# Reordering one iteration of a banded attention loop: P·V and x^T ahead of layer norm and weight conversion, a weight's halves behind the transposes' eviction, and 1e-9 added on ScalarE

## The chip, the cores and the metric

The kernel runs on one core of a Trainium2 chip. The metric is the device time of one execution in microseconds (us). The engines are TensorE (PE in the rows; PEld is its weight load), VectorE (DVE), ScalarE (ACT), GpSimd (POOL) and SyncE (SP), which issues nearly all DMAs. Each runs its own instructions strictly in the order in which the program lists them.

## The reference

Three steps follow one another, for 2 batches, 768 positions and a model width of 512:

```python
scores = scale * np.matmul(q, k.transpose(0, 1, 3, 2))        # 8 heads of 64
scores = np.where(is_sink | in_window, scores, -1e9)           # window 128, 4 sinks
scores = scores - np.max(scores, axis=-1, keepdims=True)
a = np.exp(scores)
a = a / (np.sum(a, axis=-1, keepdims=True) + 1e-09)
x = np.matmul(a, v)                                            # -> (2, 768, 512)

h = np.maximum(x @ w_in, 0.0)                                  # d_ff 1024
u, v = h[..., :512], h[..., 512:]
v_n = (v - mean(v)) / np.sqrt(var(v) + 1e-06)
gated = u * (einsum('ts,bsd->btd', w_spatial, v_n) + b_spatial)
x = gated @ w_out

h = np.maximum(x.transpose(0, 2, 1) @ w_tok1, 0.0) @ w_tok2
u = x + h.transpose(0, 2, 1)
out = u + np.maximum(u @ w_ch1, 0.0) @ w_ch2
```

## The kernel before

The matrix products behind attention run as three products each: every operand is kept as a high half (rounded by a ScalarE copy) and a low half (the difference, on GpSimd or VectorE), and `mm3` (line 55) multiplies high·high, high·low and low·high. The weights arrive in double precision; `pump` (466) turns a 128x512 piece into single precision with three VectorE instructions (lines 481, 485, 488), and `flush` (496) makes its halves, the high one on ScalarE (499), the low one on GpSimd (500). `pump` flushes the piece converted before it.

Attention is a software pipeline, `banded` (339). Block j is 128 query rows of one batch, and group g = 2j + ph is four of its eight heads. Iteration n runs from -3 to 25 and works on several groups at once. Group n+1 has its sums inverted (`sums`, 190) and its exponentials scaled (`norm`, 239: two heads on GpSimd, two on ScalarE). Group n is transposed on TensorE into one bank `tr` (`a_transpose`) and evicted by ScalarE (aT) and VectorE (aL) (`a_out`, 271). Group n+3 gets its scores (`qk`, `scores`), and group n+2 its exponentials (`expo`, 223). Group n-1 is multiplied with the values (`pv`, 288) into the one bank `pv`, which holds a whole block. In an even iteration block j-1 is finished by `sinks_mm`, and `x_out` (325) splits it: the high half xTH on ScalarE, the low half xTL on VectorE. Only then may `pv` start the next block in that bank. The sink columns take a path of their own (`v_step`, `sink_parts`, `sinks`, and `split_vs` for the sinks' values, in iterations 1 and 13).

Everything behind attention that can start early is woven in: `step` (426) moves layer norms one stage on, `pump` converts one piece of `w_in` in each of iterations -1 to 6 (`PUMPS`), and `fill` (433) puts up to about 1900 ns of later matmuls behind each iteration on TensorE, as soon as the x^T that they read is written and only in the iteration after that. The order of calls in the loop is the order on each engine:

```python
if n in (1, 13):
    self.split_vs(n // 12)
self.step()
if n in PUMPS:
    self.pump()
...
if 0 <= n - 1 < NG:
    self.pv(n - 1)
    if ph == 0:
        ...
        self.x_out(j - 1)
```

Attention ends near 143 us; `mlp` (663) follows with the leftover fills, the spatial product, and the token and channel MLPs.

Of the kernel before, what the change touches and what calls it, by code (L numbers as in the profile page):

```python
# [8 lines left out]
F32R = mybir.dt.float32r  # L9
I32 = mybir.dt.int32  # L10
U32 = mybir.dt.uint32
AF = mybir.ActivationFunctionType
ALU = mybir.AluOpType
PSUM = bass.MemoryType.PSUM

P = 128
B, H, S, D = 2, 8, 768, 64
NB = S // P
DM = H * D
# [5 lines left out]
SK = 8  # L25
SR = 3 * 4 * SK
# [3 lines left out]
NG = B * NB * 2  # L30
# [6 lines left out]
def f32(ap):  # L37
    return ap.bitcast(F32)


class Kernel:
# [106 lines left out]
            nc.sync.dma_start(out=raw[0:SR], in_=self.vs[b])  # L148
            self.vsraw = raw

    def split_vs(self, b):

        nc = self.nc
        raw = self.vsraw
        t = self.vsb[b] = self.ap.tile([P, DM], F32R, name="vs", tag="vs", bufs=1)
        nc.scalar.activation(out=t[0:SR], in_=raw[0:SR], func=AF.Copy)
        r = slice(4 * SK, 8 * SK)
        nc.vector.tensor_tensor(out=t[r], in0=raw[r], in1=f32(t[r]), op=ALU.subtract)

    def slots(self, j):  # L160

# [28 lines left out]
    def sums(self, g):  # L190

        V = self.nc.vector
        r = self.ap.tile([P, 4], F32, name="r", tag="r", bufs=3)
        self.rs[g] = r
        V.tensor_scalar(out=r, in0=self.sm[g], scalar1=1e-9, scalar2=None, op0=ALU.add)
        V.reciprocal(r, r)

    def scores(self, g):

# [23 lines left out]
    def expo(self, g):  # L223
        nc = self.nc
        j, ph = divmod(g, 2)
        i = j % NB
        u = KW if i else P
        s, nm = self.ss[g]
        if ph == 0:
            self.e[j] = self.ap.tile([P, H, KW], F32, name="e", tag="e", bufs=2)  # L230
        sm = self.ap.tile([P, 4], F32, name="sums", tag="sums", bufs=3)
        self.sm[g] = sm
        for c in range(4):
            nc.scalar.activation(  # L234
                out=self.e[j][:, 4 * ph + c, :u], in_=s[:, c, :u], func=AF.Exp, bias=nm[:, c : c + 1], scale=-1.0,
                accum_out=sm[:, c : c + 1],
            )

    def norm(self, g):

        nc = self.nc
        j, ph = divmod(g, 2)
        r = self.rs[g]
        w = KW if j % NB else P
        e = self.e[j][:, 4 * ph : 4 * ph + 4, 0:w]
        nc.gpsimd.tensor_tensor(
            out=e[:, 2:4], in0=e[:, 2:4], in1=r[:, 2:4].unsqueeze(2).to_broadcast([P, 2, w]), op=ALU.mult
        )
        for c in range(2):
            nc.scalar.activation(out=e[:, c], in_=e[:, c], func=AF.Copy, scale=r[:, c : c + 1])  # L250

    def sink_parts(self, j):

# [85 lines left out]
    def banded(self):  # L339
        self.q, self.vb, self.vsb, self.ps_s, self.ss, self.e, self.sm, self.rs = {}, {}, {}, {}, {}, {}, {}, {}  # L340
        self.aT, self.ps_x, self.aS, self.dv, self.eS = {}, {}, {}, {}, {}
        NJ = B * NB
        self.kr = self.ap.tile([P, NC4, RING, KW], F32, name="kr")
        self.vf = self.ap, "vf", 2
        self.scalar_loads(self.cp)
        self.load_qk(0, 2)
        self.warm(10)
        self.load_qk(1)
        self.prefetch()
        self.load_v(0)  # L350
        self.load_qk(2)
        self.masks(self.ap)
        for n in range(-LQ, NG + 2):
            j, ph = divmod(n, 2)
            self.xdone = self.xnext
            if ph and n >= -1:
                if (n + 7) // 2 < NJ:
                    self.load_qk((n + 7) // 2)
                if (n + 3) // 2 < NJ:
                    self.load_v((n + 3) // 2)  # L360
            if 0 <= n + LN < NG:
                self.sums(n + LN)
            if 0 <= n < NG:
                self.a_transpose(n)
                self.a_out(n)
            if 0 <= n + LN < NG:
                self.norm(n + LN)
            if n + LQ < NG:
                self.qk(n + LQ)
                if n < 0:  # L370
                    self.warm(3)
                self.scores(n + LQ)
            if 0 <= n + LE < NG:
                self.expo(n + LE)
            if 0 <= n < NG and ph == 0 and j % NB:
                self.v_step(j)
                self.sink_parts(j)
            if n in (1, 13):
                self.split_vs(n // 12)
            self.step()  # L380
            if n in PUMPS:
                self.pump()
            if n == max(PUMPS) + 1:
                self.flush()
            if 0 <= n - 1 < NG:
                self.pv(n - 1)
                if ph == 0:
                    if (j - 1) % NB:
                        self.sinks_mm(j - 1)

                    self.fill_until(j - 1)
                    self.x_out(j - 1)
            if 0 <= n < NG and ph == 1 and j % NB:
                self.sinks(j)
            if n == NG - 4:
                self.raws = [self.spatial_load(r) for r in range(2)]
            self.fill(BUDGET)
        self.xdone = self.xnext
        self.vf = self.sp, "tmp", 4
# [529 lines left out]
```

## Time and profile before

| | before |
|---|---|
| median of 3 runs | 494.08 us (492.68 to 495.11) |
| profiled execution, its own time | 494.1 us |
| its span, first to last instruction | 492.3 us |
| PE busy | 469.2 us (95%) |
| PEld busy | 392.3 us (80%) |
| DVE busy | 281.2 us (57%) |
| ACT busy | 178.8 us (36%) |
| POOL busy | 146.7 us (30%) |
| mean granted TensorE clock | 0.979 |

The profile lists the busy time of each engine by stretch, the chain of work that ended last (followed back from the end to what released each step), groups of instructions by line, and a timeline. A row of the timeline has start, duration, engine, line, operation, tiles written and read, and in brackets the idle time ahead of it with its releaser. A granted clock of 1.00 is 2.4 GHz, 0.50 is 1.2 GHz. 1.8 us of the profiled execution lie outside the span.

### The profile page before, as it was taken

To read this page: it belongs to the slowest core of one execution; us is meant where nothing else is said; L and a number is where in the kernel's file an instruction comes from. 1 tells how busy PE (TensorE), PEld (TensorE's weight loads), DVE (VectorE), ACT (ScalarE), POOL (GpSimd) and SP (SyncE) were. 2 spreads that over 40 slices of the span, in tenths; PEclk is the share of its full clock that TensorE was granted. 3 is DMA by queue.
4 is the path that set the end of the run, shared out by engine and by line. 5 is a ranking of instruction groups with operands and counts; after the bars stand their busy time and mean duration, and the time that the engine had idled before them with its cause. 6 is when DMAs were issued, how large, how long until landed. Compare 5 with 4: busy or idle time off the path is not lost.

```text
span 492.3 us, 6952 instructions
## 1 busy us (share of the span) xinstructions
PE 469.2 (95%) x2562; PEld 392.3 (80%) x2562; DVE 281.2 (57%) x633; ACT 178.8 (36%) x483; POOL 146.7 (30%) x164
## 2 busy tenths in 40 slices
PE   8678899999999999999999989999999999999994
PEld 7356588788898999998888768888888888888883
DVE  5899865775555399937878698666412211311112
ACT  4656777787754323225642122222101210010000
POOL 1355752354354556642543033222100000000000
PEclk9859899999999999999999999999999999999998
DMA  8744132202005023303534044222010000200002
GB/s 258 246 151 152 66 101 95 87 22 87 1 30 185 1 85 87 102 6 116 173 119 137 35 129 128 91 94 73 21 66 1 0 1 0 86 1 0 1 0 92
DMA packets 19722, 38.48 MB, mean 78 GB/s; under 512 B 1824, under 2 KB 8224, under 8 KB 19680
## 3 DMA queue, kind: packets, MB, share of 16 engines
q1 hardware_dynamic: 19248, 37.69, 23.5%
q8 instruction: 22, 0.36, 0.3%
q10 hardware_dynamic: 432, 0.26, 0.2%
q14 instruction: 20, 0.16, 0.1%
HBM read 34.80 MB, written 3.15 MB: 77 GB/s over the span
## 4 chain that ended last, share of the span: by engine, by line
PE 81%; DVE 11%; ACT 5%; issue 1%; POOL 1%; POOLq 0%; ACTq 0%
PE pso L60 7%; PE pso L58 7%; PE pso L59 7%; PE psc L58 6%; PE psc L60 6%; PE psc L59 6%; PE psg L60 3%; PE psg L59 3%; PE psg L58 3%; PE pv L301 3%; PE ps L60 2%; PE ps L58 2%; PE ps L59 2%; ACT e L234 2%; DVE wi L485 2%; PE psu L58 2%
## 5 line engine op out<-in xcount | busy, mean ns | idle before, releaser
L647 DVE SCALAR_TENSOR_TENSOR hh<-psc,hh 128x512 fp32r<-128x512 f32 x36 | 24.9, 691 | 124.6 <-ACT hh L646 124.6
L646 ACT ACTIVATE hh<-psc 128x512 fp32r<-128x512 f32 x36 | 21.5, 597 | 156.0 <-PE psc L60 156.0
L60 PE MATMUL pso<-c2H,hh 128*128 128x512 f32 x144 | 56.3, 391 | 1.9 <-DVE hh L647 1.9
L58 PE MATMUL pso<-c2H,hh 128*128 128x512 f32 x144 | 56.8, 394 | 0.0
L59 PE MATMUL pso<-c2L,hh 128*128 128x512 f32 x144 | 56.1, 390 | 0.0
L488 DVE SCALAR_TENSOR_TENSOR wi<-rawi,wi 128x512 int32<-128x512 int32 (+2 forms) x46 | 40.3, 876 | 1.6
L234 ACT ACTIVATE e<-s,nm 128x136 f32<-128x136 f32 (+1 forms) x96 | 37.6, 393 | 3.9 <-DVE nm L218 3.9
L485 DVE SCALAR_TENSOR_TENSOR wi<-rawi,wi 128x512 int32<-128x512 int32 (+2 forms) x46 | 36.4, 791 | 1.6
L481 DVE TENSOR_SCALAR wi<-rawi 128x512 int32<-128x512 int32 (+2 forms) x46 | 33.4, 726 | 0.7 <-DMA rawi<-in_moe_w_ch 0.5
L60 PEld LDWEIGHTS pso<-c2H,hh 128*128 128x128 f32 x144 | 27.0, 188 | 8.0 <-DVE hh L647 2.3
L58 PE MATMUL psg<-wsTH,vnH 128*128 128x384 f32 x96 | 32.1, 334 | 0.0
L59 PE MATMUL psg<-wsTL,vnH 128*128 128x384 f32 x96 | 32.1, 334 | 0.0
L60 PE MATMUL psg<-wsTH,vnL 128*128 128x384 f32 x96 | 32.1, 334 | 0.0
L500 POOL TENSOR_TENSOR c2L<-wi,c2H 128x512 fp32r<-128x512 f32 x12 | 16.1, 1339 | 52.4 <-ACT c2H L499 52.4
L59 PEld LDWEIGHTS pso<-c2L,hh 128*128 128x128 f32 x144 | 27.1, 188 | 5.4
L58 PEld LDWEIGHTS pso<-c2H,hh 128*128 128x128 f32 x144 | 27.0, 188 | 5.3
L188 PE MATMUL sc<-kr,q 64*128 64x264 f32 (+2 forms) x192 | 28.8, 419 | 0.4 <-DVE nm L218 0.2
L60 PE MATMUL psc<-u2H,c 128*128 128x512 f32 x72 | 28.0, 389 | 0.0
L58 PE MATMUL psc<-u2H,c1H 128*128 128x512 f32 x72 | 28.0, 389 | 0.0
L59 PE MATMUL psc<-u2L,c1H 128*128 128x512 f32 x72 | 28.0, 389 | 0.0
L60 PE MATMUL psc<-u2H,c1L 128*128 128x512 f32 x72 | 28.0, 389 | 0.0
L58 PE MATMUL psc<-u2H,c 128*128 128x512 f32 x72 | 28.0, 389 | 0.0
(143 smaller groups left out, 1120.1 us busy)
## 6 DMA issues: line engine op xcount, KB each, us to landing
rawi<-in_moe_w_ch SPq DMA_DIRECT2D x24, 512.0 KB, 3.4
rawi<-in_moe_w_in SPq DMA_DIRECT2D x8, 512.0 KB, 4.5
v<-in_v SPq DMA_DIRECT2D x12, 256.0 KB, 3.6
out_x<-o SPq DMA_DIRECT2D x12, 256.0 KB, 2.4
kr<-in_k SPq DMA_DIRECT2D x11, 272.0 KB, 4.1
q<-in_q SPq DMA_DIRECT2D x11, 256.0 KB, 4.2
raws<-in_w_spT SPq DMA_DIRECT2D x6, 384.0 KB, 4.5
rawi<-in_moe_w_out SPq DMA_DIRECT2D x4, 512.0 KB, 5.2
```

Of the source, the lines that this page charges most:

```text
L58: self.nc.tensor.matmul(ps, lh, rh, start=(first and i == 0), stop=False)
L59: self.nc.tensor.matmul(ps, lh, rl, start=False, stop=False)
L60: self.nc.tensor.matmul(ps, ll, rh, start=False, stop=(last and i == n - 1))
L188: nc.tensor.matmul(o, q[r, p, :], k, start=True, stop=True)
L234: nc.scalar.activation(out=self.e[j][:, 4 * ph + c, :u], in_=s[:, c, :u], func=AF.Exp, bias=nm[:, c : c + 1], scale=-1.0, accum_out=sm[:, ...
L301: nc.tensor.matmul(ps[h * D : (h + 1) * D, p, :], w[:, (2 * p + h) * D : (2 * p + h + 1) * D], self.aT[g][c][:, 2 * x + h, :], start=(p == ...
L481: V.tensor_scalar(out=wi, in0=hi, scalar1=3, scalar2=0x3FFFFFFF, op0=ALU.logical_shift_left, op1=ALU.bitwise_and,)
L485: V.scalar_tensor_tensor(out=wi, in0=hi, scalar=-0x40000000, in1=wi, op0=ALU.bitwise_and, op1=ALU.bitwise_or)
L488: V.scalar_tensor_tensor(out=wi, in0=lo, scalar=29, in1=wi, op0=ALU.logical_shift_right, op1=ALU.bitwise_or)
L500: self.nc.gpsimd.tensor_tensor(out=dl, in0=w, in1=f32(dh), op=ALU.subtract)
L646: nc.scalar.activation(out=h, in_=ps, func=AF.Relu)
L647: nc.vector.scalar_tensor_tensor(out=l, in0=ps, scalar=0.0, in1=f32(h), op0=ALU.max, op1=ALU.subtract)
```

## The change

Four things in one iteration, all in `banded` and its helpers:

- `pv(n-1)`, `sinks_mm` and `x_out` stand ahead of `v_step`, `sink_parts`, `split_vs`, `step` and `pump`, instead of behind them.
- The piece converted in iteration n-1 is flushed right behind `a_out` and the GpSimd part of `norm`, ahead of the ScalarE part of `norm`; `pump` then finds nothing to flush.
- `sums` is the reciprocal alone; the 1e-9 is added by a ScalarE copy with a bias at the end of `expo`.
- `split_vs` is in two parts: ScalarE's in iterations 2 and 14, VectorE's in 3 and 15.

```diff
-    def split_vs(self, b):
+    def split_vs(self, b, part):
...
-        t = self.vsb[b] = self.ap.tile([P, DM], F32R, name="vs", tag="vs", bufs=1)
-        nc.scalar.activation(out=t[0:SR], in_=raw[0:SR], func=AF.Copy)
-        r = slice(4 * SK, 8 * SK)
-        nc.vector.tensor_tensor(out=t[r], in0=raw[r], in1=f32(t[r]), op=ALU.subtract)
+        if part == 0:
+            t = self.vsb[b] = self.ap.tile([P, DM], F32R, name="vs", tag="vs", bufs=1)
+            nc.scalar.activation(out=t[0:SR], in_=raw[0:SR], func=AF.Copy)
+        else:
+            t = self.vsb[b]
+            r = slice(4 * SK, 8 * SK)
+            nc.vector.tensor_tensor(out=t[r], in0=raw[r], in1=f32(t[r]), op=ALU.subtract)
...
-        V.tensor_scalar(out=r, in0=self.sm[g], scalar1=1e-9, scalar2=None, op0=ALU.add)
-        V.reciprocal(r, r)
+        V.reciprocal(r, self.sm[g])
...
+        nc.scalar.activation(out=sm, in_=sm, func=AF.Copy, bias=1e-9)
...
             if 0 <= n + LN < NG:
-                self.norm(n + LN)
+                self.norm(n + LN, "P")
+            if n - 1 in PUMPS:
+                self.flush()
+            if 0 <= n + LN < NG:
+                self.norm(n + LN, "A")
             if n + LQ < NG:
...
                 self.expo(n + LE)
-            if 0 <= n < NG and ph == 0 and j % NB:
-                self.v_step(j)
-                self.sink_parts(j)
-            if n in (1, 13):
-                self.split_vs(n // 12)
-            self.step()
-            if n in PUMPS:
-                self.pump()
-            if n == max(PUMPS) + 1:
-                self.flush()
             if 0 <= n - 1 < NG:
                 self.pv(n - 1)
...
                     self.x_out(j - 1)
+            if 0 <= n < NG and ph == 0 and j % NB:
+                self.v_step(j)
+                self.sink_parts(j)
+            if n in (2, 3, 14, 15):
+                self.split_vs(n // 12, n % 2)
+            self.step()
+            if n in PUMPS:
+                self.pump()
```

The order on TensorE and on the DMA queues does not change. Three places where it does, as the built programs list it.

VectorE, from the last scores of iteration 2 to the first transposes' low copy of iteration 3, before:

```order
L218 ISA s,nm<-sc,m_141 128x136
L218 ISA nm 128x1
L481 TENSOR_SCALAR wi<-rawi 128x512
L485 SCALAR_TENSOR_TENSOR wi<-rawi,wi 128x512
L488 SCALAR_TENSOR_TENSOR wi<-rawi,wi 128x512
L330 TENSOR_TENSOR xTL<-pv,xTH 128x4x128
L195 TENSOR_SCALAR r<-sums 128x4
L196 RECIPROCAL r<-r 128x4
L278 TENSOR_TENSOR aL<-tr,lowT 128x512
```

and now:

```order
L220 ISA s,nm<-sc,m_141 128x136
L220 ISA nm 128x1
L335 TENSOR_TENSOR xTL<-pv,xTH 128x4x128
L488 TENSOR_SCALAR wi<-rawi 128x512
L492 SCALAR_TENSOR_TENSOR wi<-rawi,wi 128x512
L495 SCALAR_TENSOR_TENSOR wi<-rawi,wi 128x512
L198 RECIPROCAL r<-sums 128x4
L283 TENSOR_TENSOR aL<-tr,lowT 128x512
```

The low half of x^T (xTL) has moved ahead of the three conversions, and the addition ahead of the reciprocal is gone.

ScalarE in iteration 4 (aT is the transposes' eviction, wuH a weight's high half, e<-e,r the scaling, sums the exponentials' sums), before:

```order
L275 ACTIVATE aT<-tr 128x512
L250 ACTIVATE e<-e,r 128x136 x2
L234 ACTIVATE e,sums<-s,nm 128x136 x4
L257 ACTIVATE eS<-e 128x2x32
L499 ACTIVATE wuH<-wi 128x512
L329 ACTIVATE xTH<-pv 128x4x128
L532 ACTIVATE vf<-psv 128x512
```

and now:

```order
L280 ACTIVATE aT<-tr 128x512
L506 ACTIVATE wuH<-wi 128x512
L255 ACTIVATE e<-e,r 128x136 x2
L236 ACTIVATE e,sums<-s,nm 128x136 x4
L240 ACTIVATE sums<-sums 128x4
L334 ACTIVATE xTH<-pv 128x4x128
L262 ACTIVATE eS<-e 128x2x32
L539 ACTIVATE vf<-psv 128x512
```

The weight's high half has moved from behind the exponentials to ahead of the scaling, the addition of 1e-9 is new, and xTH stands ahead of the sinks' copy eS.

GpSimd in iteration 2 (e<-e,r is its part of the scaling, dv the difference of two value blocks, wvL a weight's low half), before:

```order
L246 TENSOR_TENSOR e<-e,r 128x272
L285 TENSOR_TENSOR dv<-v 128x512
L258 CAST eS<-eS 128x2x32
L259 TENSOR_TENSOR eS<-e,eS 128x2x32
L500 TENSOR_TENSOR wvL<-wi,wvH 128x512
```

and now:

```order
L250 TENSOR_TENSOR e<-e,r 128x272
L507 TENSOR_TENSOR wvL<-wi,wvH 128x512
L290 TENSOR_TENSOR dv<-v 128x512
L263 CAST eS<-eS 128x2x32
L264 TENSOR_TENSOR eS<-e,eS 128x2x32
```

The weight's low half is now second in the iteration instead of last; in odd iterations GpSimd's order stays as it was.

## Rows read from the trace of the kernel before

**Rows 1.** Busy time by stretch: us, each engine's busy us (instructions), granted clock, DMA share, GB/s.

```profile
10.00:60.00 50.00, 37.93 (x253) 26.48 (x252) 46.62 (x148) 32.90 (x119) 26.04 (x30) 0.83 0.51 168
20.00:35.00 15.00, 10.73 (x54) 7.12 (x55) 13.42 (x45) 10.32 (x38) 6.92 (x9) 0.54 0.47 157
60.00:150.00 90.00, 89.16 (x696) 73.75 (x695) 53.39 (x206) 64.07 (x214) 40.68 (x60) 1.00 0.20 66
```

**Rows 2.** Pieces of the chain that ended last: start, us, what.

```profile
31.10 1.98 PE pv L301 x16
...
54.53 0.61 DVE xTL L330
55.18 1.85 PE pv L301 x16
...
60.27 0.44 PE tr L267 x4
```

**Rows 3.** TensorE's longest wait between 9 and 60 us: us, times, longest.

```profile
PE pv L301 <- DVE xTL L330: 4.2, 3, 1.6
```

**Rows 4.** Line 195 alone, by stretch: us, VectorE's busy us (instructions), granted clock, DMA.

```profile
14.00:54.50 40.50, 2.65 (x7) 0.83 0.52 171
```

**Rows 5.** Groups by line on VectorE, 9 to 60 us: count, busy us, mean ns, idle.

```profile
L488 DVE SCALAR_TENSOR_TENSOR wi<-rawi,wi 128x512 int32<-128x512 int32 x8 | 7.5, 935 | 0.3
L485 DVE SCALAR_TENSOR_TENSOR wi<-rawi,wi 128x512 int32<-128x512 int32 x8 | 6.5, 815 | 0.3
...
L481 DVE TENSOR_SCALAR wi<-rawi 128x512 int32<-128x512 int32 x8 | 4.5, 559 | 0.0
```

**Rows 6.** The same eight conversions by tile: duration ns min/median/max.

```profile
L481 DVE TENSOR_SCALAR wi<-rawi x8: 421/426/1427, 12.3 to 52.6; 128x512 int32<-128x512 int32 x8
L485 DVE SCALAR_TENSOR_TENSOR wi<-rawi,wi x8: 691/692/1658, 12.8 to 53.1; 128x512 int32<-128x512 int32 x8
L488 DVE SCALAR_TENSOR_TENSOR wi<-rawi,wi x8: 691/693/1676, 13.5 to 53.8; 128x512 int32<-128x512 int32 x8
```

**Rows 7.** Timeline, 17 to 28 us: GpSimd beside VectorE.

```profile
17.48 1.75 POOL L500 TENSOR_TENSOR wvL<-wi,wvH 128x512 fp32r<-128x512 f32 x1 [2.19 <-ACT wvH L499]
...
18.02 1.23 DVE L195 TENSOR_SCALAR r<-sums 128x4 f32<-128x4 f32 x1
...
22.39 0.68 DVE L158 TENSOR_TENSOR vs<-vsraw,vs 32x512 fp32r<-32x512 f32 x1 [1.13 <-ACT vs L156]
...
26.95 1.27 POOL L285 TENSOR_TENSOR dv<-v 128x512 f32<-128x512 f32 x1
...
27.22 0.30 DVE L218 CUSTOM_DVE_ANT_0 s<-sc,m 128x136 f32<-128x136 f32 x1
```

**Rows 8.** Timeline of iteration 4 on ScalarE and VectorE.

```profile
37.09 0.18 DVE L196 RECIPROCAL r<-r 128x4 f32<-128x4 f32 x1
37.36 0.71 ACT L250 ACTIVATE e<-e,r 128x136 f32<-128x136 f32 x2
37.98 0.39 ACT L234 ACTIVATE e<-s,nm 128x136 f32<-128x136 f32 x1
...
39.54 0.24 ACT L257 ACTIVATE eS<-e 128x64 fp32r<-128x64 f32 x1
39.69 0.62 ACT L499 ACTIVATE wuH<-wi 128x512 fp32r<-128x512 f32 x1
39.87 0.49 DVE L481 TENSOR_SCALAR wi<-rawi 128x512 int32<-128x512 int32 x1
40.21 0.57 ACT L329 ACTIVATE xTH<-pv 128x512 fp32r<-128x512 f32 x1
```

**Rows 9.** Timeline: TensorE's longest idle time between 60 and 150 us.

```profile
69.29 0.44 PE L58 MATMUL psu<-xTH,wuH 128*128 128x384 f32 x1 [0.57 <-ACT aS L313]
```

**Rows 10.** Timeline of TensorE, 26 to 31 us: transposes and scores of iteration 3.

```profile
26.99 1.09 PE L267 MATMUL tr<-ident,e 128*128 128x128 f32 x4 [3.29 <-DVE aL L278]
28.01 2.13 PE L188 MATMUL sc<-kr,q 64*128 64x264 f32 x8
```

More of the change, by code (lines that the diff above doesn't have):

```diff
@@ L237, in expo, with norm @@
             )
-    def norm(self, g):
+        nc.scalar.activation(out=sm, in_=sm, func=AF.Copy, bias=1e-9)
+    def norm(self, g, on):
         nc = self.nc
@@ L245, in norm @@
         e = self.e[j][:, 4 * ph : 4 * ph + 4, 0:w]
[L246 to L250, printed above, removed]
+        if on == "P":
+            nc.gpsimd.tensor_tensor(
+                out=e[:, 2:4], in0=e[:, 2:4], in1=r[:, 2:4].unsqueeze(2).to_broadcast([P, 2, w]), op=ALU.mult
+            )
+        else:
+            for c in range(2):
+                nc.scalar.activation(out=e[:, c], in_=e[:, c], func=AF.Copy, scale=r[:, c : c + 1])
     def sink_parts(self, j):
```

## The prediction, made before the changed kernel ran

> **What bounds the kernel now.** I read busy time by stretch first, then the chain of waits, then the timeline where the chain changes engine. By stretch [rows 1], TensorE works 89.2 of the 90 us from 60 to 150, so there it is the bound and nothing that other engines save can show. From 10 to 60 us it works 37.9 of 50, while VectorE works 46.6 of 50: the early attention iterations are VectorE's, and TensorE has no other work yet, since the products behind attention need x^T. The clock says the same: between 20 and 35 us the granted clock is 0.54, mostly the lower of the two levels, 1.2 GHz. The chain of waits [rows 2] runs mostly over VectorE up to 54.53 us, where VectorE writes the third low half of x^T (xTL); that releases the bank `pv`, and TensorE takes over at 55.18 with the next block's products with the values. From its transposes at 60.27 TensorE has work without end. TensorE's longest wait before that is of this kind: `pv` for xTL, three times, 4.2 us [rows 3].
>
> So the question is by how much the third xTL, the one of iteration 6, comes earlier. From there TensorE needs 60.27 - 54.53 = 5.7 us to the point where it is saturated, and the rest of its work follows unchanged, because its order is unchanged.
>
> **The change part by part**, on VectorE's path up to that xTL (iterations 0 to 6).
>
> *1e-9.* Line 195 goes. Seven of its instructions lie on the path and take 2.65 us [rows 4]. They are 128x4 elements; one took 1.23 us, from 18.02 to 19.25, while GpSimd's low half of a weight ran from 17.48 to 19.23 [rows 7]. VectorE stood still until GpSimd was done. The reciprocal now comes first in the iteration and could stand still in its place; then little more than the 7 x 0.16 = 1.1 us of unhindered ones would be saved (0.16 is an estimate from the reciprocal's 0.18 [rows 8], with the same shape). But GpSimd's work moves too (next part), so I take **-2.65**, bounds -1.1 and -2.65.
>
> *A weight's halves behind the eviction.* The eight conversions take 7.5 + 6.5 + 4.5 = 18.5 us [rows 5]; unhindered, by their medians, 8 x (0.693 + 0.692 + 0.426) = 14.5 [rows 6]. So 4.0 us are standing still, in single instructions of 1.4 to 1.7 us, and the cause is the one above: GpSimd subtracts the last weight while VectorE converts the next. In the changed order GpSimd subtracts right after its part of the scaling, while VectorE evicts transposes and masks scores. There the two do not hinder each other: dv on GpSimd took 1.27 and the masking beside it 0.30 [rows 7], the time of dv elsewhere. Behind the weight's low half GpSimd has dv (1.27) and the sinks, and later a layer norm's low half, and these reach into the conversions of iterations 2, 4 and 6; I give back 0.5. **-3.5**, bounds 0 (it stays, beside another instruction) and -4.0.
>
> *Sinks' values in two parts.* VectorE waited 1.13 us for ScalarE [rows 7]; with an iteration between the parts the wait goes, the 0.68 of work stays: **-1.1**.
>
> *x^T ahead of the conversion.* The conversion of iteration 6 (0.426 + 0.692 + 0.693 [rows 6]) now lies behind the third xTL: **-1.8** for TensorE. But VectorE works in order, so xTL in front of the conversion waits for xTH, where before the conversion filled that time. In iteration 4 [rows 8] scaling began 0.27 after the reciprocal, took 0.62, the exponentials 1.56. Now the weight's high half (39.69 to 40.21: 0.52) stands ahead of the scaling, and it cannot start before the last conversion, which ends about where the reciprocal starts. So xTH starts 0.1 + 0.52 + 0.62 + 1.56 + the addition after the reciprocal, and ends 0.57 later. The addition on ScalarE is new: the nearest row is the sinks' copy, 0.24 long with the next instruction 0.15 behind it; an exponential (1.56 / 4 = 0.39) bounds it above, 0.1 below; I take 0.2, near the small copy. xTH ends 3.6 after the reciprocal, while VectorE is free after 39.87 - 37.09 = 2.8, less 0.2 if nothing keeps its eviction waiting: a wait of 0.8 to 1.0. Three times: **+3.0**, bounds 2.1 and 4.0.
>
> The Trainium skill speaks against putting the addition there: ScalarE: Activation LUTs, "Rules for kernel authors", sends adds to VectorE and budgets about 0.3 us for an ACTIVATE, with a pointer as bias (the bias here is a constant). By that figure the three additions on the path would cost 0.3 us more in all, an estimate from that page; the trace shows no ACTIVATE of this shape.
>
> Sum to the third xTL: -2.65 - 3.5 - 1.1 - 1.8 + 3.0 = -6.05.
>
> *What is late next.* TensorE comes 6 us earlier, VectorE less: the conversion and layer norm of iteration 6 still stand ahead of its next reciprocal. In iteration 9 TensorE waited 0.57 us for the sinks' eviction aS, which ScalarE does behind the exponentials [rows 9]; it now finds aS behind the addition as well, and behind a scaling that is released later relative to it. I put **+0.6** there, bounds 0 and 1.5. Later additions lie on ScalarE, which works 64 of 90 us from 60 to 150 [rows 1], and cost nothing while TensorE is the bound there. dv behind a weight costs nothing: it is read an iteration later. The DMA queues keep their order.
>
> Net -5.45: the profiled execution took 494.1 us, as the median of the runs (494.08), so **488.6 us**.
>
> **The rivals.**
>
> *VectorE keeps the pace (490.5).* If not the 5.7 us of TensorE's work but VectorE's next reciprocal and ScalarE's scaling set the time of the saturation, the 1.8 us of the conversion behind xTL are no gain: 494.1 - 4.25 + 0.6 = 490.5. For it: TensorE ran part of these 5.7 us at the lower clock, as `pv` with 1.85 beside 1.98 shows [rows 2], and could be faster, hence waiting again. Against it: 5.7 us hold the 0.6 of xTL, 1.8 of conversion and 0.9 to the end of the scaling with room to spare. Chance 0.17.
>
> *The standing still stays (493.7).* If GpSimd holds VectorE up wherever its work is put, or the reciprocal inherits it, only 1.1 of the first part and nothing of the second are gained: -1.1 - 1.1 - 1.8 + 3.0 + 0.6 = -0.4. Against it: dv beside the masking [rows 7]. Chance 0.11.
>
> *TensorE makes x^T late (496.7, slower).* xTH needs this iteration's `pv`, behind its transposes and scores on TensorE. At 1.2 GHz these took 1.02, 2.13 and 1.98 us to the next start or end [rows 2, 10], with the sinks' product (about 0.6, an estimate from `pv`'s four-matmul share) 5.7. If TensorE reaches its transposes only with the reciprocal, xTH starts 5.7 after it instead of 3.0 and VectorE, in order, stands still 2.7 us more in each of three iterations: +8.1 on 488.6. It decides where `pv` ends over 3.0 us after the reciprocal. Against it: in an even iteration little stands ahead of the transposes, which wait only for the scaling one iteration before. Chance 0.06.
>
> *No second wait (486.9).* TensorE runs its 5.7 us at 2.4 GHz (0.8 less), the 0.6 of iteration 9 does not come, and the addition costs 0.1: -1.7 more. Chance 0.12.
>
> **How the numbers follow.** The forecast has 0.54; its own range is 487.2 to 490. The range 486.0 to 492.0 takes in the first rival and most of the last, and leaves out the second and third and a little of the last, 0.2. What a measurement can tell from no change is about 0.5%, 2.5 us: faster by more means under 491.6. Nearly all of the forecast, most of the first rival and all of the last lie there: 0.78. Within 0.5% lie the second rival and the tails: 0.17. Slower: 0.05.
>
> **What would show it.** No conversion over 1.2 us except beside a layer norm's low half; reciprocals of 0.18; xTL in iterations 2, 4 and 6 with an idle time of 0.7 to 1.4 released by xTH, the third at about 48.5; the transposes now at 60.27 near 54; busy time of TensorE unchanged after 60, and its idle time gone from before. The prediction is wrong if the conversions still stand still, if xTL waits over 2 us, or if TensorE's wait for aS grows beyond 2 us.

## The result and the profile after

The changed kernel takes **488.17 us** (median of 5 runs, 488.04 to 490.38) against 494.08: a ratio of 0.9895 (95% interval 0.9866 to 0.9923), 5.9 us less. The forecast was 488.6, and the time lies in its own range. Its profiled execution took 488.14 us, span 486.4. TensorE was busy 465.6 us of it (96%), VectorE 273.9, ScalarE 183.2, GpSimd 143.5, and the mean granted clock was 0.993.

Line numbers have moved: the sums' reciprocal is L198, xTH and xTL are L334 and L335, the three conversion instructions L488, L492 and L495, a weight's halves L506 and L507, dv L290, aT and aL L280 and L283, the sinks' eviction aS L318, the addition of 1e-9 L240. First busy time by stretch, the view of [rows 1] (columns as there: busy us of PE, PEld, DVE, ACT, POOL, then the granted clock, DMA share, GB/s):

```profile
10.00:60.00 50.00, 41.29 (x303) 27.93 (x301) 44.08 (x152) 39.48 (x144) 26.75 (x36) 0.97 0.56 185
14.00:20.00 6.00, 5.17 (x30) 3.41 (x32) 5.76 (x26) 5.72 (x23) 3.72 (x4) 0.72 1.03 322
60.00:150.00 90.00, 88.64 (x672) 73.45 (x671) 51.48 (x182) 63.55 (x213) 38.69 (x58) 1.00 0.22 74
```

From 10 to 60 us TensorE does 3.4 us more than before and VectorE 2.5 less; from 60 on TensorE is saturated as it was. The clock is the other difference: before it was 0.54 from 20 to 35 us [rows 1], now it is 1.00 there, and its one fall lies between 14 and 20 us.

Iterations 5 and 6 up to the third xTL, timeline of VectorE, ScalarE and GpSimd, the rows that answer to [rows 7, 8]:

```profile
42.40 0.41 DVE L488 TENSOR_SCALAR wi<-rawi 128x512 int32<-128x512 int32 x1
42.85 0.69 DVE L492 SCALAR_TENSOR_TENSOR wi<-rawi,wi 128x512 int32<-128x512 int32 x1
43.58 0.69 DVE L495 SCALAR_TENSOR_TENSOR wi<-rawi,wi 128x512 int32<-128x512 int32 x1
44.19 0.17 DVE L198 RECIPROCAL r<-sums 128x4 f32<-128x4 f32 x1
44.30 0.63 ACT L506 ACTIVATE wuH<-wi 128x512 fp32r<-128x512 f32 x1 [1.54 <-DVE wi L495]
45.04 1.28 POOL L507 TENSOR_TENSOR wuL<-wi,wuH 128x512 fp32r<-128x512 f32 x1
45.75 0.42 DVE L215 COPY_PREDICATED sc<-up,sc 128x256 f32<-128x256 uint32 x1
46.28 1.26 POOL L290 TENSOR_TENSOR dv<-v 128x512 f32<-128x512 f32 x1
47.13 0.21 ACT L240 ACTIVATE sums<-sums 128x4 f32<-128x4 f32 x1
47.25 0.58 ACT L334 ACTIVATE xTH<-pv 128x512 fp32r<-128x512 f32 x1
47.86 0.69 DVE L335 TENSOR_TENSOR xTL<-pv,xTH 128x512 fp32r<-128x512 f32 x1 [1.12 <-ACT xTH L334]
48.57 1.45 POOL L558 TENSOR_TENSOR vnL<-vf,vnH 128x512 fp32r<-128x512 f32 x1
48.92 1.65 DVE L492 SCALAR_TENSOR_TENSOR wi<-rawi,wi 128x512 int32<-128x512 int32 x1
```

The conversions take their unhindered time, and so does GpSimd (1.28 and 1.26) beside the masking. The reciprocal takes 0.17. xTL waits 1.12 us for xTH, in each of iterations 2, 4 and 6, and the third one comes at 47.86, 6.6 us before its old 54.45. One conversion still stands still, at 48.92, beside a layer norm's low half, as the prediction allowed; it lies behind the third xTL. TensorE behind it, its transposes of iteration 8 and its waits for aS:

```profile
52.90 0.41 PE L272 MATMUL tr<-ident,e 128*128 128x128 f32 x2 [0.76 <-DVE aL L283]
53.75 0.44 PE L272 MATMUL tr<-ident,e 128*128 128x128 f32 x2 [0.44 <-POOL e L250]
63.39 0.44 PE L58 MATMUL psu<-xTH,wuH 128*128 128x384 f32 x1 [1.04 <-ACT aS L318]
73.81 0.44 PE L58 MATMUL psu<-xTH,wuH 128*128 128x384 f32 x1 [0.32 <-ACT aS L318]
```

They are the transposes that stood at 60.11 to 60.27 [rows 2], so TensorE reaches them 7.2 us earlier. The wait of 0.44 for GpSimd's scaling in the middle of them is new, and the wait for aS, 0.57 before [rows 9], is 1.36 in two, which takes 0.8 back: 6.0 are left.

### The profile page after: what moved, and what is told of

Its sections match the earlier page's. It is cut to its first block, busy times and chain, and to the rows that moved or that the text cites. A ratio compares the mean times of both kernels' runs of the same rounds, so it can differ in the third digit from the quotient of the medians.

```text
span 486.4 us, 6920 instructions
## 1 busy us (share of the span) xinstructions
PE 465.6 (96%) x2562; PEld 387.9 (80%) x2562; DVE 273.9 (56%) x609; ACT 183.2 (38%) x507; POOL 143.5 (30%) x164
## 4 chain that ended last, share of the span: by engine, by line
PE 81%; DVE 10%; ACT 6%; issue 1%; DMA 1%; POOL 0%; POOLq 0%; ACTq 0%
PE pso L60 7%; PE pso L58 7%; PE pso L59 7%; PE psc L60 6%; PE psc L58 6%; PE psc L59 6%; PE psg L60 3%; PE psg L59 3%; PE psg L58 3%; PE pv L306 3%; PE sc L191 2%; ACT e L236 2%; PE ps L60 2%; PE ps L58 2%; PE ps L59 2%; DVE wi L492 2%
## 5 line engine op out<-in xcount | busy, mean ns | idle before, releaser
L495 DVE SCALAR_TENSOR_TENSOR wi<-rawi,wi 128x512 int32<-128x512 int32 (+2 forms) x46 | 39.2, 853 | 1.6
L492 DVE SCALAR_TENSOR_TENSOR wi<-rawi,wi 128x512 int32<-128x512 int32 (+2 forms) x46 | 37.4, 813 | 1.6
L488 DVE TENSOR_SCALAR wi<-rawi 128x512 int32<-128x512 int32 (+2 forms) x46 | 31.4, 682 | 1.6 <-DMA rawi<-in_moe_w_ch 0.9
L507 POOL TENSOR_TENSOR c2L<-wi,c2H 128x512 fp32r<-128x512 f32 x12 | 15.9, 1321 | 52.7 <-ACT c2H L506 52.7
```

The source lines that it names most:

```text
L488: V.tensor_scalar(out=wi, in0=hi, scalar1=3, scalar2=0x3FFFFFFF, op0=ALU.logical_shift_left, op1=ALU.bitwise_and,)
L492: V.scalar_tensor_tensor(out=wi, in0=hi, scalar=-0x40000000, in1=wi, op0=ALU.bitwise_and, op1=ALU.bitwise_or)
L495: V.scalar_tensor_tensor(out=wi, in0=lo, scalar=29, in1=wi, op0=ALU.logical_shift_right, op1=ALU.bitwise_or)
L507: self.nc.gpsimd.tensor_tensor(out=dl, in0=w, in1=f32(dh), op=ALU.subtract)
```

## The experiments

Twelve kernels ran, E1 to E12 in the order in which the expectations count them, in three groups of four, each group beside the kernel before on the same chip. Ratios are to that, with their 95% interval; its median was 493.59, 494.05 and 494.07 in the three groups (the third on another chip than the first two), so that a difference of two medians from different groups carries half a microsecond of that. The changed kernel was not run again in them: every difference to its 488.17 below is of this kind, and its five runs span 2.3 us, so the positions in the traces are the firmer evidence. The theory on trial is the prediction's ledger. The first rival: not the standing still but x^T's halves ahead of the conversion make the gain. T(8) is the start of TensorE's transposes of iteration 8.

| run | median (runs), us | profiled, us | third xTL | T(8) | clock 20 to 60 us |
|---|---|---|---|---|---|
| before | 494.08 (492.68 to 495.11) | 494.1 | 54.45 | 60.11 | 0.79 |
| changed | 488.17 (488.04 to 490.38) | 488.14 | 47.86 | 52.90 | 1.00 |
| E1 halves early alone | 492.15 (491.7 to 494.57) | 492.42 | 52.26 | 57.91 | 0.84 |
| E2 x^T ahead alone | 495.84 (495.3 to 496.97) | 496.97 | 54.49 | 60.72 | 0.83 |
| E3 changed, x^T behind | 490.61 (489.42 to 491.01) | 491.01 | 50.12 | 55.78 | 0.87 |
| E4 changed, halves late | 492.91 (491.97 to 495.52) | 492.8 | 50.25 | 56.28 | 0.89 |
| E5 E3 and idle matmuls | 487.88 (487.28 to 489.69) | 487.58 | 48.36 | 52.46 | 1.00 |
| E6 before and idle matmuls | 494.10 (491.82 to 495.83) | 493.47 | 53.15 | 57.71 | 0.96 |
| E7 changed, 1e-9 on VectorE | 488.98 (487.8 to 490.19) | 487.93 | 47.81 | 53.05 | 1.00 |
| E8 changed, conversion split | 487.41 (486.77 to 488.81) | 486.77 | 46.91 | 51.50 | 1.00 |
| E9 changed and idle matmuls | 489.83 (488.02 to 490.08) | 489.85 | 47.85 | 52.89 | 1.00 |
| E10 E8, 1e-9 late | 486.28 (485.9 to 487.46) | 486.28 | 46.56 | 51.13 | 0.96 |
| E11 E10 and idle matmuls | 487.89 (487.52 to 487.94) | 487.85 | 46.60 | 51.32 | 1.00 |
| E12 E11, hh ahead | 483.84 (483.64 to 484.41) | 483.64 | 46.57 | 51.29 | 1.00 |

### E1: a weight's halves early, alone

```diff
 # before, plus
-                self.norm(n + LN)
+                self.norm(n + LN, "P")
+            if n - 1 in PUMPS:
+                self.flush()
+            if 0 <= n + LN < NG:
+                self.norm(n + LN, "A")
```

Expected:

> The kernel before with one part of the change alone: a weight's halves right behind GpSimd's part of the scaling, ahead of ScalarE's. The theory of the ledger: this part carries most of the gain, because GpSimd's subtraction no longer stands beside VectorE's conversions (4.0 us of standing still) nor beside the addition of 1e-9 on VectorE (7 x 1.23 less 7 x 0.16 would be more than was there; 2.65 - 1.1 = 1.55). With the conversion still ahead of x^T, xTL waits for nobody. So single conversions near their medians, no addition over 0.3 us, the third xTL near 54.5 - 5 = 49.5 us, and about 489.3 us in all. The rival (x^T's halves ahead of the conversion are what releases TensorE earlier and so carry the gain): the standing still goes but the third xTL comes hardly earlier, since ScalarE's scaling now starts 0.5 later in each iteration and the whole chain with it; about 493 us.

Measured: ratio 0.9976 (0.9958 to 0.9994). VectorE's groups from 8 to 64 us:

```profile
L485 DVE TENSOR_SCALAR wi<-rawi 128x512 int32<-128x512 int32 x8 | 5.8, 720 | 0.0
L492 DVE SCALAR_TENSOR_TENSOR wi<-rawi,wi 128x512 int32<-128x512 int32 x8 | 5.5, 692 | 0.3
L489 DVE SCALAR_TENSOR_TENSOR wi<-rawi,wi 128x512 int32<-128x512 int32 x8 | 5.5, 692 | 0.3
L195 DVE TENSOR_SCALAR r<-sums 128x4 f32<-128x4 f32 x11 | 1.7, 155 | 0.0
```

Its longest wait from 9 to 62 us (total, times, longest):

```profile
DVE aL L280 <- ACT aT L277: 3.5, 2, 2.0
```

The two long conversion instructions and the addition no longer stand still: the addition now takes 0.155 us each, before it was 2.65 us in seven [rows 4]. The first one, L485, does (0.72 instead of 0.42, 2.4 us in eight): dv on GpSimd now runs beside it, for 0.98 to 1.26 in iterations 2, 4 and 6. So the eight conversions still take 16.8 us of the 18.5, and the third xTL comes only 2.2 us earlier, not 5; 492.15 lies nearer the rival's 493 than the ledger's 489.3. VectorE also waits 3.5 us for aT, the transposes' eviction on ScalarE: 1.5 ahead of the third xTL, where it was 0.2 before, and 2.0 behind it. Neither was in the expectation, and the next runs are about them.

### E2: x^T ahead, alone

```diff
 # before, plus
+            if 0 <= n - 1 < NG:
+                self.pv(n - 1)
...
+                    self.x_out(j - 1)
             if 0 <= n < NG and ph == 0 and j % NB:
                 self.v_step(j)
```

Expected:

> The kernel before with one part alone: weights times values and x^T's halves ahead of the conversion and layer norm. The theory of the ledger: the conversion of iteration 6 goes behind the third xTL (-1.8 us), and VectorE then waits for xTH in each of three iterations, by less than in the changed kernel since neither the weight's high half nor the addition stands ahead of the scaling on ScalarE: 0.3 to 0.6 us each, 1.0 to 1.8 together; the standing still of the conversions stays. Third xTL 0 to 1 us earlier, 493 to 494 us in all. The rival (x^T ahead is what carries the gain): third xTL 3 us or more earlier, about 490 us.

Measured: ratio 1.0047 (1.0028 to 1.0065), slower by 2.2 us; the third xTL stands where it stood (54.49), at the edge of what the ledger said, and the total is 2 us worse than it said. With the halves still late, GpSimd's work stands beside the conversion of each even iteration: one of its instructions stands still in iterations 2 and 4 (1.65 us), and two in iteration 6, beside a layer norm's low half and a weight's low half. Timeline of iteration 6, VectorE and GpSimd:

```profile
54.49 0.69 DVE L330 TENSOR_TENSOR xTL<-pv,xTH 128x512 fp32r<-128x512 f32 x1 [0.51 <-ACT xTH L329]
55.20 1.45 POOL L551 TENSOR_TENSOR vnL<-vf,vnH 128x512 fp32r<-128x512 f32 x1
55.55 1.65 DVE L485 SCALAR_TENSOR_TENSOR wi<-rawi,wi 128x512 int32<-128x512 int32 x1
56.61 1.76 POOL L500 TENSOR_TENSOR wuL<-wi,wuH 128x512 fp32r<-128x512 f32 x1
57.23 1.68 DVE L488 SCALAR_TENSOR_TENSOR wi<-rawi,wi 128x512 int32<-128x512 int32 x1
...
59.82 0.18 DVE L196 RECIPROCAL r<-r 128x4 f32<-128x4 f32 x1
```

The reciprocal behind them was at 56.95 before, so VectorE comes 2.9 us later into iteration 7, and T(8) waits 1.96 us for aL. The rival in its simple form falls: x^T ahead alone is a loss.

### E3: the change without x^T ahead

```diff
 # changed kernel, minus
-            if 0 <= n - 1 < NG:
-                self.pv(n - 1)
...
-                    self.x_out(j - 1)
             if 0 <= n < NG and ph == 0 and j % NB:
                 self.v_step(j)
 # and put back behind pump()
```

Expected:

> The changed kernel without one part: weights times values and x^T's halves stand behind the conversion and layer norm again. The theory of the ledger: VectorE no longer waits for xTH (3 x 1.12 = 3.4 us gone), the conversion of iteration 6 stands ahead of the third xTL again (+1.8): third xTL near 46.3 us where the changed kernel has 47.86; VectorE reaches the reciprocal of iteration 7 earlier too, and TensorE's waits for the sinks' eviction aS (1.36 us in two) shrink. 485 to 487 us in all, 1.5 to 3 under the changed kernel. The rival (x^T ahead carries the gain): third xTL and the end later by the 1.8 of the conversion, 489.5 to 490.5 us.

Measured: ratio 0.9923 (0.9902 to 0.9944), 2.4 us above the changed kernel. Here the ledger is plainly wrong and the rival's number nearly right (490.61, for 489.5 to 490.5): the third xTL is at 50.12, not 46.3. First the conversions' first instruction (VectorE's groups, 8 to 64 us), in this kernel and in the changed one. Then this kernel's waits of TensorE and of VectorE from 9 to 62 us, the two longest of TensorE for xTL in the timeline, and busy time by stretch (the third row is of TensorE alone):

```profile
L488 DVE TENSOR_SCALAR wi<-rawi 128x512 int32<-128x512 int32 x8 | 5.6, 706 | 0.0
```

```profile
L488 DVE TENSOR_SCALAR wi<-rawi 128x512 int32<-128x512 int32 x8 | 3.6, 445 | 0.0
```

```profile
PE pv L306 <- DVE xTL L335: 5.6, 3, 2.4
DVE aL L283 <- ACT aT L280: 3.6, 2, 2.2
```

```profile
27.48 0.69 PE L306 MATMUL pv<-aT,v 128*64 128x128 f32 x4 [2.06 <-DVE xTL L335]
50.85 0.44 PE L306 MATMUL pv<-aT,v 128*64 128x128 f32 x4 [2.36 <-DVE xTL L335]
```

```profile
24.00:31.00 7.00, 4.84 (x29) 3.32 (x26) 6.80 (x22) 5.99 (x22) 4.13 (x5) 0.55 0.71 225
51.00:56.00 5.00, 5.00 (x29) 4.02 (x28) 3.71 (x16) 2.75 (x12) 4.09 (x7) 0.66 0.01 2
24.00:26.00 2.00, 1.32 (x8) 0.69 0.79 245
```

Two things stand against the ledger's 46.3. First, where VectorE no longer waits for xTH it runs into dv: the first conversion instruction takes 1.17, 0.98 and 1.20 us in iterations 2, 4 and 6, unhindered 0.42, which gives 2.1 of the 3.4 us back. In the changed kernel dv runs while VectorE waits for xTH, and costs nothing.

Second, the clock. It falls to 0.5, the lower level, twice: near 24.8 us and near 52 us. The matmuls that follow take 0.63 us each instead of 0.39, so the transposes come late, aT with them, and VectorE waits for it, 1.4 us ahead of the third xTL and 2.2 behind it. TensorE stands 2.06 and 2.36 us before the first and the third `pv`, in the changed kernel 1.0, with the clock at 1.00 in these stretches and a wait of 0.2 for aT. But only the second fall follows such a stand (TensorE goes on at 50.85). At the first, TensorE had stood 1.3 us twice since 17.8, and the stand of 2.06 begins only at 25.4. The changed kernel stands 1.3 us near 22 too and keeps its clock there. What starts the first fall is not shown.

### E4: the change with the halves late

```diff
 # changed kernel, minus
-                self.norm(n + LN, "P")
-            if n - 1 in PUMPS:
-                self.flush()
-            if 0 <= n + LN < NG:
-                self.norm(n + LN, "A")
+                self.norm(n + LN)
```

Expected:

> The changed kernel without one part: a weight's halves stand behind the exponentials again, as before the change. The theory of the ledger: GpSimd's subtraction stands beside the conversions or beside what follows the reciprocal again, 3.5 to 4 us up to the third xTL; the reciprocal itself may stand still in place of the addition (up to 7 x 0.2 more); xTL waits for xTH 0.5 to 0.7 instead of 1.12 each, since the weight's high half no longer stands ahead of the scaling (-1.3). Sum +2.5 to +3.5: 490.5 to 492 us. The rival (x^T ahead carries the gain): within 1 us of the changed kernel, 487.5 to 489.

Measured: ratio 0.9975 (0.9957 to 0.9994), 4.7 us above the changed kernel; the ledger had 2.5 to 3.5. The second and third conversion instructions (VectorE's groups, 8 to 64 us), and then the third xTL in the timeline:

```profile
L488 DVE SCALAR_TENSOR_TENSOR wi<-rawi,wi 128x512 int32<-128x512 int32 x8 | 9.5, 1189 | 0.3
L491 DVE SCALAR_TENSOR_TENSOR wi<-rawi,wi 128x512 int32<-128x512 int32 x8 | 7.5, 937 | 0.3
```

```profile
50.25 0.69 DVE L333 TENSOR_TENSOR xTL<-pv,xTH 128x512 fp32r<-128x512 f32 x1 [0.69 <-ACT xTH L332]
```

Unhindered these two take 5.5 us each (E1), so 6.0 us of standing still are back, where the kernel before had 4.0 in all three [rows 5, 6]: x^T ahead makes it worse, as in E2. The waits of 0.66 to 0.69 are as expected. No reciprocal took over 0.18: it did not inherit the standing still.

### E5 and E6: the clock held by idle matmuls

```diff
 # E5: the kernel of E3, E6: the kernel before, plus
             if 0 <= n < NG:
+                if n in (1, 2, 3):
+                    self.warm(8)
                 self.a_transpose(n)
...
             if 0 <= n - 1 < NG:
+                if n in (3, 5, 7):
+                    self.warm(8)
                 self.pv(n - 1)
```

Expected of E5:

> The kernel of the third run above (the change without weights times values and x^T ahead) with idle matmuls on TensorE, which nobody reads: eight ahead of the transposes of iterations 1, 2 and 3 and eight ahead of the products with the values of iterations 3, 5 and 7, where TensorE waited. The clock theory: that kernel lost its gain because TensorE, waiting 2.1 and 2.4 us for xTL, found the clock at 0.5 when it went on (26 to 31 and 52 to 55 us), so that transposes and their eviction aT came late and VectorE waited 3.6 us for aT. With the idle matmuls the granted clock is 1.00 from 20 to 60 us, the waits for aT fall under 1 us, the third xTL comes at 47.5 to 48.5 us instead of 50.12, and 487 to 488.5 us in all. The rival (the order itself: the bank of x^T is given back too late, whatever the clock): waits for aT and the third xTL within 0.7 us of that kernel, 490 to 491 us.

Expected of E6:

> The kernel before with the same idle matmuls on TensorE, and no part of the change. If most of the change's gain is the clock (before, it was at 0.5 from 21 to 35 and from 56 to 59 us): clock 1.00 there, 489 to 490 us. By the ledger of the prediction, VectorE's standing still and the additions of 1e-9 set the pace and TensorE's clock only the 1.3 us in which VectorE waited for aT and the last stretch behind the third xTL (5.7 us of TensorE's work at the lower clock): third xTL 0.5 to 1.5 us earlier, 491.5 to 493 us.

E5 measured: ratio 0.9889 (0.9858 to 0.9920); as the clock theory said, and 2.7 us under E3, with forty-eight matmuls more to do. The stretches that E3 spent largely at the lower level, then the waits from 9 to 62 us:

```profile
24.00:31.00 7.00, 6.86 (x57) 5.50 (x55) 6.76 (x19) 5.39 (x20) 3.72 (x5) 1.00 0.67 217
51.00:56.00 5.00, 5.00 (x42) 3.86 (x41) 4.24 (x21) 4.58 (x21) 3.57 (x4) 1.00 0.08 8
```

```profile
PE pv L306 <- DVE xTL L335: 0.2, 1, 0.2
DVE aL L283 <- ACT aT L280: 1.0, 2, 0.7
```

The order was E3's, the clock was not, and the wait for aT fell from 3.6 to 1.0, all of it behind the third xTL. The third xTL came 1.8 us earlier than in E3 and T(8) 3.3. Of both, 0.5 is there at the first conversion (11.89 for 12.40), ahead of the first added matmul and of E3's first fall, so the clock had cost E3 some 1.3 us at the third xTL, about its wait for aT there, and 2.8 at T(8). The standing still beside dv stayed: 1.19, 1.19 and 1.20 us in iterations 2, 4 and 6.

E6 measured: ratio 1.0007 (0.9987 to 1.0028), no change; the ledger's forecast was nearer than the clock's, and still too low. In the profiled execution the third xTL came 1.3 us earlier, as the ledger said, and T(8) 2.4. The additions took what they had taken, the conversions 17.4 us instead of 18.5, since one instruction (1.65 before, 0.69 here) no longer met GpSimd. The clock was not wholly held: from 24 to 31 us it is 0.78. The execution gave 1.7 of that back far behind, near 290 us (see E9); whether its other executions did is not shown. In the kernel before, then, this much of the clock is worth some 2.4 us at T(8), and 1.0 of that is the one conversion; a clock held throughout was not tried there.

### E7: 1e-9 back on VectorE

```diff
 # from the changed kernel
+        V.tensor_scalar(out=r, in0=self.sm[g], scalar1=1e-9, scalar2=None, op0=ALU.add)
+        V.reciprocal(r, r)
-        V.reciprocal(r, self.sm[g])
...
-        nc.scalar.activation(out=sm, in_=sm, func=AF.Copy, bias=1e-9)
```

Expected:

> The changed kernel with the addition of 1e-9 back on VectorE. In the first run above the addition took 0.155 us each where the weight's halves stood early, so 1.55 of the 2.65 us that the prediction gave this part belong to the weight's halves. By the ledger: 7 x 0.155 = 1.1 us more on VectorE up to the third xTL, less 0.24 in each of three waits for xTH, which comes that much earlier behind the reciprocal: third xTL 0.3 to 0.5 us later than in the changed kernel, the wait for the sinks' eviction aS 0.2 shorter, 488 to 489 us. The rival (the addition on ScalarE is dear, as a budget of 0.3 us each would have it, and gives back all it saves): 487 to 488 us. A third: the addition takes 1.2 us again, 490 us.

Measured: ratio 0.9907 (0.9876 to 0.9939); its profiled execution is 0.2 us under the changed kernel's, its median 0.8 above: no difference that these runs can tell. The third xTL is at 47.81, 0.05 earlier than in the changed kernel, where 0.3 to 0.5 later was expected. xTL waits 0.68 instead of 1.12 in each of three iterations, which pays 1.3 us for the seven additions of about 0.16 us. With the halves early, this part of the change is worth nothing.

### E8 and E10: filling the wait for xTH, and 1e-9 later

```diff
 # E8: changed kernel; pump in two parts, in even iterations
+                    if n in PUMPS:
+                        self.pump_a()      # the first of the three instructions
                     self.x_out(j - 1)
...
+                    self.pump_b()          # the other two
 # E10: E8, and at the end of the iteration instead of in expo
+            if 0 <= n + LE < NG:
+                self.eps(n + LE)           # sums + 1e-9 on ScalarE
```

Expected of E8:

> The changed kernel with one step more: in iterations 2, 4 and 6 the first of the conversion's three instructions (0.42 us) stands ahead of x^T's low half, in the 1.12 us that VectorE waits for xTH. If it fits there, although GpSimd's dv runs beside it and may hold it up to 1.0 us: xTL not later, its wait 0.2 to 0.7 us, the next reciprocal 0.4 earlier in each of three iterations, third xTL near 47.0 us, 487.2 to 487.8 us in all. The rival: the instruction stands still beside dv and pushes xTL back, TensorE waits longer for it and meets the lower clock again as without x^T ahead: 489 to 490.5 us.

Expected of E10:

> The eighth run's kernel (first conversion instruction ahead of x^T's low half) with ScalarE's addition of 1e-9 at the end of the iteration, behind xTH, the sinks' copy and the sinks' eviction aS, instead of right behind the exponentials. It leaves the stretch ahead of xTH (0.24 us in each of iterations 2, 4 and 6) and ahead of aS. If ScalarE's chain sets xTH and aS: xTH 0.2 earlier each, third xTL 0.1 to 0.4 earlier than that run's 46.91, TensorE's wait for aS 0.2 shorter, 486.6 to 487.3 us. The rival: dv on GpSimd still holds the first conversion instruction and so xTL, or the reciprocal now waits for the late addition: 487.2 to 488.5 us.

E8 measured: ratio 0.9878 (0.9849 to 0.9908), as expected; E10 0.9845 (0.9829 to 0.9861), 0.3 us under what was expected, which is less than two groups differ by. In E8 the instruction stands beside dv and takes 1.19 us, about what xTL waited, and xTL follows xTH without a wait. Timeline of iteration 6, GpSimd and VectorE:

```profile
45.33 1.28 POOL L290 TENSOR_TENSOR dv<-v 128x512 f32<-128x512 f32 x1
45.71 1.19 DVE L501 TENSOR_SCALAR wi<-rawi 128x512 int32<-128x512 int32 x1
46.91 0.69 DVE L335 TENSOR_TENSOR xTL<-pv,xTH 128x512 fp32r<-128x512 f32 x1
```

What follows xTL is 0.42 shorter for it, in iterations 2 and 4 ahead of the third xTL, which comes 0.95 earlier. E10 gains another 0.35 there, and TensorE's wait for aS falls from 1.4 us in two to 0.6 in one.

### E9, E11 and E12: the fall near 288 us

```diff
 # E9: changed kernel, E11: E10, plus the idle matmuls of E5, five instead of eight
 # E12: E11, and in mlp
-            if n >= 9:
+            if 9 <= n < 11:
                 pump()
...
                 self.ch1_tile(ch, f)
                 if ch == 0:
                     pump()
+                if n == 0:
+                    pump()
```

Expected of E9:

> The changed kernel with idle matmuls on TensorE at the places of the fifth run, five instead of eight, since TensorE waits only 1.0 us for xTL here. The clock theory: the clock stays at 1.00 from 10 to 60 us (the changed kernel's one fall, 15 to 20 us, lies where VectorE sets the pace), and nothing else changes: third xTL 47.5 to 48.0 us, 487.3 to 488.3 us in all. Then x^T ahead of the conversion is worth, where the clock is held anyway, no more than 0.5 us against the fifth run's 487.88. The rival (x^T ahead is worth something of its own, since TensorE gets its bank back 0.5 to 1.8 earlier): 485.5 to 487 us.

Expected of E11:

> The tenth run's kernel with five idle matmuls on TensorE at the places of the ninth. The eighth run's clock was at 1.00 from 10 to 60 us in the profiled execution already, but its runs lie at mean clocks of 0.989 and 0.996. If the low ones are falls in the early iterations: the runs lie closer together, 486 to 487 us in the middle. If they are the fall behind TensorE's wait of 1.9 us for hh near 288 us: the spread stays, and the middle is that of the tenth run within 0.5 us.

Expected of E12:

> The eleventh run's kernel with one conversion of a weight more behind the first channel tile's hidden layer instead of ahead of it, far behind the change: near 285 us, the first low half of hh stood behind that conversion (1.68 + 0.69 us) on VectorE, and TensorE waited 1.90 us for it, in before and in the changed kernel. If the wait goes: 1.5 to 1.9 us less, and without the fall of the clock behind it the spread of the runs (about 2 us) goes as well: 484 to 485.5 us. If the wait only moves to the next tile's weight: 486 to 487 us.

E9 measured: ratio 0.9895 (0.9875 to 0.9914), at 489.83 above both forecasts. From the first xTL to T(8) it is the changed kernel to 0.03 us, clock 1.00 throughout, as the clock theory said. The 1.7 us come at the other end. Both kernels let TensorE wait 1.9 us for VectorE's hh near 285 us; busy time of TensorE behind it, with the granted clock, first the changed kernel, then E9:

```profile
284.00:286.00 2.00, 0.13 (x1) 1.00 0.40 162
286.00:288.00 2.00, 2.00 (x9) 1.00 0.67 238
288.00:290.00 2.00, 2.00 (x10) 1.00 0.23 82
```

```profile
284.00:286.00 2.00, 0.15 (x1) 1.00 0.40 162
286.00:288.00 2.00, 2.00 (x5) 0.50 0.81 227
288.00:290.00 2.00, 2.00 (x7) 0.65 0.35 68
```

At half speed for 3.4 us TensorE loses 1.7 us (2 x 0.5 + 2 x 0.35), and 489.85 - 1.7 is the changed kernel's 488.14. Two of E9's five runs, with a mean clock of 0.997 instead of 0.992, took 488.02 and 488.38. E11 (ratio 0.9869, 0.9854 to 0.9884) shows the same fall in its profile and lies 1.6 us above E10; its runs do lie closer together (0.4 us), but not at the 486 to 487 expected, so it came out in none of the two ways. E6 showed the fall at 290 us. So what E9 and E11 lose, they lose there and not in attention. Whether the idle matmuls, far ahead of it, make this fall likelier is open: three of the four profiles that have them and this wait show it (E5 does not), and none of the nine without them.

E9 and E5 also show what x^T ahead is worth with the clock held in both, one execution each: the third xTL comes 0.5 us earlier with it (47.85 for 48.36), T(8) 0.4 later (52.89 for 52.46), and the end 0.6 later (488.15, less the fall, for 487.58).

E12 takes the wait away: one conversion goes behind hh. Ratio **0.9794** (0.9780 to 0.9807), the runs within 0.8 us, 10.2 us under the kernel before and 4.3 under the changed one. E11's waits of TensorE over the whole span show the line that E12's do not have:

```profile
PE pso L60 <- DVE hh L684: 1.9, 1, 1.9
```

E12 from 284 to 290 us, all engines:

```profile
284.00:287.00 3.00, 3.00 (x15) 2.47 (x14) 2.86 (x4) 1.34 (x4) 1.61 (x2) 1.00 0.54 175
287.00:290.00 3.00, 3.00 (x15) 2.46 (x14) 2.93 (x4) 0.56 (x2) 1.42 (x1) 1.00 0.66 175
```

Between E11 and E12 lie 4.0 us: 1.9 of the wait, 1.7 of the clock (the fall in E11's profile), and 0.4 that the profile does not name.

## Why the prediction was right, and where it was not

- **The bound.** TensorE from 60 us on, VectorE before: right. The third xTL moved by 6.6 us (6.05 forecast), the end by 5.9 to 6.0 (5.45). Added up from the rows of both kernels, its parts come to -6.1: line 195 -2.65, the conversions ahead of it -5.7 (18.5 before, 12.8 of 15.6 now), the sinks' values -1.1, the waits for xTH +3.4. The other 0.4 is there at the first of these conversions (11.94 for 12.35); E3, whose VectorE order is the changed kernel's up to there, has 12.40, so it may be chance.
- **1e-9 (-2.65).** The time of line 195 is gone and the reciprocal inherited nothing. But 1.55 of it belongs to the halves (E1: 0.155 each is left), and the remaining 1.1 VectorE spends in longer waits for xTH (E7). With the halves early it is worth nothing as a part; the sum was right because both parts were made. As sized, the new addition on ScalarE was right: xTH begins 0.33 us behind the start of the last read of an accumulator, 24.00 to 24.33, where ScalarE's next instruction otherwise follows after 0.09, so it costs 0.24 where 0.2 was taken. The Trainium skill, ScalarE: Activation LUTs, "Rules for kernel authors", budgets about 0.3 us for an ACTIVATE, a little more than that, and sends adds to VectorE: E7 did so and lost nothing that can be measured.
- **The halves (-3.5).** Right in mechanism: E1 and E4 show the standing still of the two long instructions go and come. The eight conversions take 15.6 us (3.6 + 6.5 + 5.5) instead of 18.5 [rows 5], with one standing still behind the third xTL. But the size needs x^T ahead: in E1 and E3 dv takes 2.4 and 2.1 us of it back. The 0.5 that the prediction gave back for dv and what follows it was too little for this part by itself, and more than the 0.2 that was lost ahead of the third xTL in the whole change. The Trainium skill, SBUF — State Buffer, "Who interferes with whom", says that a VectorE instruction with two SBUF inputs contends with a GpSimd instruction that reads SBUF, that the port pair they share is an exclusive lock, and that the issue order decides who blocks. The rows agree: GpSimd's 1.45 at 48.57 ends at 50.02, and VectorE's 1.65 at 48.92, unhindered 0.69, ends 0.55 behind it. The masking takes its 0.42 at 45.75 inside GpSimd's 1.28 from 45.04, and E4's reciprocals at 17.49 and 21.16 take 0.17 inside GpSimd's low halves of 1.59 from 17.13 and 20.81.
- **Sinks' values (-1.1).** The wait of 1.13 [rows 7] is gone from every kernel with this part and is 1.1 to 1.3 in E1, E2 and E6. It was not tried alone.
- **x^T ahead (-1.8 + 3.0).** This is the step that failed. The waits are as forecast, 3 x 1.12 = 3.4. But the ledger says that the change would be better by 1.2 us without this part, and E3 shows it 2.4 us worse, the third xTL 2.3 later. The +3.0 counts VectorE's waits for xTH as lost, and they are not: dv runs in them, and without them a conversion stands still beside it for 2.1 (E3) to 2.3 us (E5). The ledger also left TensorE's clock as it was, and without this part the clock falls and costs some 1.3 us at the third xTL (E3 against E5). With the clock held in both (E5, E9), this part is worth 0.5 us at the third xTL, the ledger's own point, and costs 0.6 at the end. That it keeps the clock up by cutting TensorE's stand before `pv` from 2.1 and 2.4 us to 1.0 is argued for the second fall and not shown for the first. And alone it makes the standing still worse (E2), so the parts do not add: E1 gives -1.4, E2 +2.2, both in the change with the others -5.9.
- **Give-back (+0.6).** 0.8 measured, most of it at the place named.
- **"VectorE keeps the pace".** Partly true: T(8) waits for aL and, half done, for GpSimd's scaling (0.76 and 0.44). TensorE's stretch to it fell from 5.66 us to 5.04, at the full clock, so TensorE did get faster, as that rival said, and met VectorE again.

The prediction read the clock of 0.54 and priced it only in two rivals, not in its ledger. E6, which held it in part, puts 2.4 us of the kernel before on it at T(8). So the total was right with some luck: the parts were priced one by one, and they do not add.

## What to carry to other kernels

Before an order is priced on the busy engine, ask what another engine does in a wait that the order makes or removes: here VectorE's waits of 1.12 us hid GpSimd's dv, and without them a conversion stood still beside it. Look at the granted clock of each stretch too: one order kept it from 20 to 60 us and the other lost it twice, and the loss came back through the next eviction to the engine that was sped up. Price the parts of a change together and test them by taking one away as well as by adding one, since here one part alone was a loss, another worth nothing beside the rest, and the whole 5.9 us. Work that cannot be done earlier fits into a wait of an in-order engine (E8), and a wait of 1.9 us may be worth twice its length (E12).

## What the runs showed of the hardware that was not expected

- The same wait of 1.9 us near 285 us is followed by a clock of 0.50 in E9 and by 1.00 in the changed kernel: its length alone does not decide, and what does is open here.
- Matmuls that nobody reads cost nothing up to T(8) where TensorE waits anyway: E9 has 30 more of them than the changed kernel and reaches it within 0.01 us, and E5, with 48 more than E3, is 2.7 us faster.
- VectorE's TENSOR_SCALAR on 128x512 stands still beside GpSimd as the two-input forms do: 0.42 becomes 1.19 beside dv, which ended 0.3 us ahead of it; RECIPROCAL on 128x4 took 0.17 inside a GpSimd subtraction of 1.59 (E4, 17.49), where the addition on 128x4 had taken 1.23 [rows 7].
